# Three of the chunks' layer norms on ScalarE alone, and the first pair sums behind a product's outputs

## The chip, the cores and the metric

One core of one Trainium2 chip. The metric is the device time of one execution in microseconds (us); quoted times are medians of the runs of one kernel. The span of a profile, taken on one execution, is about 1.8 us shorter than that execution's time. Engines: PE is TensorE (PEld its weight loads), DVE is VectorE, ACT is ScalarE, POOL is GpSimd, SP is SyncE, which issues most of the DMAs here.

Some terms. A bank is one of the 8 PSUM buffers of the kernel's pool `psum`, which take PE's products; evacuating it means reading the product out, on ACT or DVE. `pg`, `pu`, `pv`, `ex` and `ey` are names of such products, `sg` is what ACT reads out of the q, k and v projection, and "a `pv` wait" is PE's wait before that product.

## The reference

A transformer block in bf16, 2048 rows of 1024, both layer norms before their part:

```python
h  = x + wo( local_attention( layernorm(x) @ wqkv ) )      # 32 heads, window 8, dilation 2
h2 = h + ( (layernorm(h) @ w_gate) * (layernorm(h) @ w_up) ) @ w_down     # w_gate, w_up: 1024 x 3584

def _layernorm(x, axis=-1, eps=1e-5):
    m = jnp.mean(x, axis=axis, keepdims=True)
    v = jnp.var(x, axis=axis, keepdims=True)
    return (x - m) / jnp.sqrt(v + eps)
```

## The kernel before: the parts that matter

The 2048 rows go through in four chunks of 512 (four tiles of 128 rows). Every engine's order is fixed by the program: `bg.step(us)` stands between PE's matmul groups and emits pieces of background work (attention and norms of other chunks), as far as a credit in microseconds allows. PE's order never changes. Chunks 2 and 3 are multiplied at the end with a scheme that needs sums and differences of weights and activations in fp16 (`weight_sums`, `activation_sums`).

A row tile's norm takes statistics on DVE, two small activations on ACT for the reciprocal deviation, a normalize on DVE and a DMA transpose that SP issues. In the output projection of a chunk that stands between the groups:

```python
lnp  = ctx.enter_context(tc.tile_pool(name="ln", bufs=4))
psum = ctx.enter_context(tc.tile_pool(name="psum", bufs=8, space=PSUM))
# ... cut ...
def stats(src, mv4, t):
    st = small.tile([128, 2, nc.vector.BN_STATS_DIM], F32, tag="st")
    for i in range(2):
        nc.vector.bn_stats(out=st[:, i, :], in_=src[:, bass.ts(i, 512)])
    nc.vector.bn_aggr(out=mv4[:, t, :], in_=st[:])

def rstd_of(mv4, rs4, lo, hi):
    nc.scalar.activation(rs4[:, lo:hi], mv4[:, lo:hi, 1], ACTF.Ln, bias=eps[:])
    nc.scalar.activation(rs4[:, lo:hi], rs4[:, lo:hi], ACTF.Exp, scale=-0.5)
# ... cut ...
def wo_ln2(c):
    lnT = lnTp.tile([128, KO, TC], BF, tag="lnT", name=f"lnT2_{c}")
    hs = hss[c]
    mv4, rs4 = ln_tiles(f"2_{c}")

    def norm(t):
        ln = normalize(hs[t], mv4, rs4, t)
        nc.sync.dma_start_transpose(lnT[:, :, bass.ts(t, 128)], ln[:])

    for t in range(4):
        for hf in range(2):
            ps = psum.tile([128, 512], F32, tag="mm", name=f"wo{c}_{hf}_{t}")
            # ... 8 matmuls into ps ...
            nc.vector.tensor_tensor(hs[t][:, bass.ts(hf, 512)], ps[:], hs[t][:, bass.ts(hf, 512)], ALU.add)
            if hf == 1:
                stats(hs[t], mv4, t)
                rstd_of(mv4, rs4, t, t + 1)
                bg.spend(1.5)
            elif t > 0:
                norm(t - 1)
                bg.spend(0.55)
            bg.spend(0.7)
            bg.step(GROUP_US)
    norm(3)
    retire(2)              # frees two weight buffers: SP issues the next two loads of 1 MB
    return lnT, hs
```

`ffn1(0, lnT2)` consumes `lnT`: its first group multiplies all 512 columns, so it waits for the last of the four transposes. The place of the pair sums, near the end of chunk 1's work:

```python
sub([dn["kx"], dn["vx"]], dn["21"], dn["11"])
weight_sums(0, nc.vector)
retire(2)
et = att.tile([128, TC], F32, tag="t3", name="et")
for q in range(2):
    dprod(ex[q], q, EF["21"], fcells(dn["12"]), False)
    nc.vector.tensor_tensor(et[:], p5t[:, q, :], hs1[2 + q][:, 512:1024], ALU.add)
    result(1, hs1[2 + q], 2 + q, 1, ex[q], dn["inv"], et)   # reads the bank ex[q] out, on DVE
retire(1)
activation_sums(l2, l3, dn["px"])
for q in range(2):
    dprod(ey[q], q, EF["12"], fcells(dn["22"]), False)
    nc.vector.tensor_tensor(p5t[:, q, :], p5t[:, q, :], hs1[q][:, 512:1024], ALU.add)
    result(1, hs1[q], q, 1, ey[q], dn["inv"], p5t[:, q, :])
for q in range(2):
    dprod(ex[q], q, EF["22"], fcells([dn["kx"], dn["vx"]]), False)
    # ... cut ...
```

Of the kernel before, what the change touches and what calls it, by code (L numbers as in the profile page):

```python
# [8 lines left out]
BF = mybir.dt.bfloat16  # L9
F32 = mybir.dt.float32  # L10
# [3 lines left out]
ACTF = mybir.ActivationFunctionType  # L14
# [4 lines left out]
D = 1024  # L19
# [6 lines left out]
TC = 512  # L26
NCH = S // TC
SUB = TC // 4
KO = D // 128
# [7 lines left out]
class Background:  # L37
# [3 lines left out]
    def __init__(self):  # L41
        self.items = []
        self.now = 0.0
        self.credit = 0.0
        self.rate = 1.0

    def add(self, gen, ready=0.0, first=False):
        self.items.insert(0 if first else len(self.items), [ready, gen])
# [3 lines left out]

    def step(self, us):
        self.now += us
        self.credit = min(self.credit + us * self.rate, 4.0)
        while self.credit > 0:
            item = next((i for i in self.items if i[0] <= self.now), None)
            if item is None:
                break
            try:  # L60
                got = next(item[1])
                if isinstance(got, tuple):
                    item[0] = self.now + got[1]
                else:
                    self.credit -= got
            except StopIteration:
                self.items.remove(item)

    def finish(self, gen):
        for item in self.items:  # L70
# [8 lines left out]
def kernel(  # L79
# [11 lines left out]
    nc = tc.nc  # L91
# [8 lines left out]
    lnTp = ctx.enter_context(tc.tile_pool(name="lnT", bufs=3))  # L100
# [21 lines left out]
    bg = Background()  # L122
# [35 lines left out]
    wts = {}  # L158
# [19 lines left out]
# [10 lines that stand above are left out]
    def normalize(src, mv4, rs4, t):  # L188
        ln = lnp.tile([128, D], BF, tag="ln")
        nc.vector.tensor_scalar(ln[:], src[:], mv4[:, t, 0:1], rs4[:, t:t + 1], ALU.subtract, ALU.mult)  # L190
        return ln

    def ln_tiles(name):
        mv4 = small.tile([128, 4, nc.vector.BN_AGGR_DIM], F32, tag="mv4", name="mv" + name)
        rs4 = small.tile([128, 4], F32, tag="rs4", name="rs" + name)
        return mv4, rs4
# [8 lines left out]

    lnTs = {}

    xtiles = {}

    class Norm1:  # L210
# [31 lines left out]
    def rows_gen(n, on_array):  # L242
        for t in range(6):
# [6 lines left out]
            if t > 1 and on_array:  # L250
                n.transpose_on_array(t - 2)
                yield 0.45

    def stats_gen(n):
        for t in range(4):
            n.stat(t)
            yield 1.5

    def norm_gen(n):
        for t in range(4):  # L260
            n.norm(t)
            n.transpose(t)
            yield 0.55


    x0 = [hp.tile([128, D], BF, tag="h", name=f"x0_{t}") for t in range(4)]
# [112 lines left out]
    xtiles[1] = load_x(1, "x", nc.sync)  # L379
    pump(4)  # L380
    xtiles[2] = load_x(2, "x", nc.sync)
    norm1 = {c: Norm1(c) for c in (1, 2, 3)}
    bg.add(rows_gen(norm1[1], True))
    rows2 = rows_gen(norm1[2], False)
    bg.add(rows2)
# [114 lines left out]
    def wo_ln2(c):  # L500
        lnT = lnTp.tile([128, KO, TC], BF, tag="lnT", name=f"lnT2_{c}")
        hs = hss[c]
        mv4, rs4 = ln_tiles(f"2_{c}")

        def norm(t):
            ln = normalize(hs[t], mv4, rs4, t)
            nc.sync.dma_start_transpose(lnT[:, :, bass.ts(t, 128)], ln[:])

        for t in range(4):
            for hf in range(2):  # L510
                ps = psum.tile([128, 512], F32, tag="mm", name=f"wo{c}_{hf}_{t}")
                for kk in range(KO):
                    nc.tensor.matmul(ps[:], lhsT=oTs[c][:, kk, t, :], rhs=wts["wo", c, hf][:, kk, :],  # L513
                                     start=(kk == 0), stop=(kk == KO - 1))
                nc.vector.tensor_tensor(hs[t][:, bass.ts(hf, 512)], ps[:], hs[t][:, bass.ts(hf, 512)], ALU.add)
                if hf == 1:
                    stats(hs[t], mv4, t)
                    rstd_of(mv4, rs4, t, t + 1)
                    bg.spend(1.5)
                elif t > 0:  # L520
                    norm(t - 1)
                    bg.spend(0.55)
                bg.spend(0.7)
                bg.step(GROUP_US)
        norm(3)
        retire(2)
        return lnT, hs

# [30 lines left out]
            nc.vector.tensor_scalar(ib[:], eb[:], float(12 << 23), None, ALU.subtract)  # L559
            self.s, self.inv = sb[:].bitcast(F32), ib[:].bitcast(F32)  # L560

    scale_gu, scale_d, scale_h = Scale("gu", 56), Scale("d", 56), Scale("h", 56)
    scale_h1 = Scale("h1", 28)

    def abs_sum(c, b, j):
# [2 lines left out]
        scale_gu.add(28 * c + 4 * b + j, wt[:, bass.ts(j, 2), :], junk[:])  # L568

    def abs_sum_down(hf, b, j):  # L570
        junk = lnp.tile([128, 512], BF, tag="ln", name=f"junkd{hf}_{b}_{j}")
        scale_d.add(28 * hf + 7 * b + j, wts["wd", 0, hf, b][:, j, :], junk[:])

    def abs_sum_h(n, k, ht):
        junk = lnp.tile([128, 512], BF, tag="ln", name=f"junkh{n}_{k}")
# [6 lines left out]
    def ffn1(c, lnT, at={}):  # L582
        hT = []
        for b in range(7):
            if b == 5 and c + 1 < NCH:
                hss[c + 1] = load_x(c + 1, "h", nc.sync)
            for j in range(4):
                pg = psum.tile([128, TC], F32, tag="mm", name=f"pg{c}_{b}_{j}")
                mm_group(pg, wts["wg", c, b], j, lnT)
                gs = t1k.tile([128, TC], BF, tag="t1k", name=f"gs{c}_{b}_{j}")  # L590
                nc.scalar.copy(gs[:], pg[:])  # L591
                bg.step(GROUP_US)
                pu = psum.tile([128, TC], F32, tag="mm", name=f"pu{c}_{b}_{j}")
                mm_group(pu, wts["wu", c, b], j, lnT)
                us = t1k.tile([128, TC], BF, tag="t1k", name=f"us{c}_{b}_{j}")
                nc.scalar.copy(us[:], pu[:])  # L596
                nc.vector.tensor_tensor(gs[:], gs[:], us[:], ALU.mult)
                abs_sum(c, b, j)
                bg.spend(0.45)
                bg.step(GROUP_US)  # L600
                hT.append(gs)
                if (b, j) in at:
                    at[b, j]()
                f = len(hT) - 3
                if c == 1 and f >= 0:
                    abs_sum_h1(f, hT[f])
            retire(2)
            if b in at:
                at[b]()
        if c == 1:  # L610
            for f in range(NF - 2, NF):
                abs_sum_h1(f, hT[f])
        return hT
# [6 lines left out]
    def ffn2(c, hf, hT, hs, between={}):  # L620
        acc = [psum.tile([128, 512], F32, tag="mm", name=f"acc{c}_{hf}_{t}") for t in range(4)]
        for b in range(4):
            for j in range(7):
                f = b * 7 + j
                for t in range(4):
                    nc.tensor.matmul(acc[t][:], lhsT=hT[f][:, bass.ts(t, 128)],  # L626
                                     rhs=wts["wd", c, hf, b][:, j, :],
                                     start=(f == 0), stop=(f == NF - 1))
                if c == 0:
                    abs_sum_down(hf, b, j)  # L630
                bg.step(0.86)
            retire()
            if b in between:
                between[b]()
        for t in range(4):
            ffn2_store(c, t, hf, acc[t], hs)
            bg.spend(0.7)
# [30 lines left out]
    def activation_sums(l2, l3, room):  # L668
        b11, b12, b21, b22 = l2[:, 0:4, :], l3[:, 0:4, :], l2[:, 4:8, :], l3[:, 4:8, :]

        t1, t2, t3, t4 = (room[:, bass.ts(i, 4), :].bitcast(F16) for i in range(4))
        nc.vector.tensor_tensor(t1, b12, b11, ALU.subtract)
        nc.vector.tensor_tensor(t2, b22, t1, ALU.subtract)
        nc.vector.tensor_tensor(t3, b22, b12, ALU.subtract)
        nc.vector.tensor_tensor(t4, b21, t2, ALU.subtract)
        pair["b"] = (b11, b21, t1, t2, t3, t4, b22)
# [56 lines left out]
        norm1[2].transpose(t)  # L733
    xtiles[3] = load_x(3, "x", nc.sync)
    pump(6)
    bg.add(stats_gen(norm1[3]), bg.now + 6.0)
    start_attention(0)
    qkv(1, range(4))
    qkv(0, range(4, 6))
    load_v(0)  # L740
    bg.add(norm_gen(norm1[3]), bg.now, first=True)
    qkv(1, range(4, 6))
    start_attention(1)
    pump(pair_at)
# [7 lines left out]
    qkv(3, range(4, 6), last=True)  # L752
    start_attention(3)
    lnT2, hs = nxt
    hT = ffn1(0, lnT2)
    bg.finish(atts[1])
    nxt = wo_ln2(1)
    for hf in range(2):
        ffn2(0, hf, hT, hs)
    lnT2, hs = nxt  # L760
    def f16(ap):
        return ap.bitcast(F16)

# [206 lines left out]
    for t in range(4):  # L970
        ln_rows(3, t, l3)
    sub([dn["kx"], dn["vx"]], dn["21"], dn["11"])
    weight_sums(0, nc.vector)
    retire(2)
    et = att.tile([128, TC], F32, tag="t3", name="et")
    for q in range(2):
# [2 lines left out]
        result(1, hs1[2 + q], 2 + q, 1, ex[q], dn["inv"], et)  # L979
    retire(1)  # L980
    activation_sums(l2, l3, dn["px"])
    for q in range(2):
        dprod(ey[q], q, EF["12"], fcells(dn["22"]), False)
        nc.vector.tensor_tensor(p5t[:, q, :], p5t[:, q, :], hs1[q][:, 512:1024], ALU.add)
        result(1, hs1[q], q, 1, ey[q], dn["inv"], p5t[:, q, :])
# [140 lines left out]
```

## Time and profile before

| | before |
|---|---|
| time, first three runs | 783.46 us median, 782.1 to 784.1 |
| profiled execution | span 779.9 us, mean granted clock 0.999 |
| PE, DVE, ACT busy | 98%, 79%, 61% of the span |
| longest wait of PE | 3.2 us, for DVE to read a bank out, at 511 |

PE is the bound. A busy share of 98% leaves 13 us of idle time in all, so this is read by place: where does PE stand still, and who ended it? An engine other than PE that stands still costs nothing by itself. The lines are in the prediction.

### The profile page before, as it was taken

How to read it: one execution, taken by the hardware profiler on the slowest of the kernel's cores; microseconds unless marked ns; L12 is line 12 of the kernel's file. 1: busy time of each engine (PE TensorE's matmuls, PEld its weight loads, DVE VectorE, ACT ScalarE, POOL GpSimd, SP SyncE). 2: the span in 40 equal slices, each digit the busy share in tenths (PEclk: the TensorE clock that was granted, in tenths of full speed). 3: DMA queues.
4: the chain of work that ended last, by engine and by line, in shares of the span. 5: the costliest groups of instructions: out<-in, count | busy, mean ns of one | idle time of the engine just before them, and what ended most of it. 6: DMA issues, size and time to landing. Idle time of an engine off the chain costs nothing.

```text
span 779.9 us, 10436 instructions
## 1 busy us (share of the span) xinstructions
PE 766.8 (98%) x3648; PEld 355.0 (46%) x3707; DVE 614.9 (79%) x805; ACT 473.5 (61%) x1028; POOL 142.4 (18%) x152
## 2 busy tenths in 40 slices
PE   8999999999999999999999999989999999999997
PEld 6544444444444444444444444434444444444444
DVE  6629999999899998999979989975553444579862
ACT  5627445313576652966769799836677677788240
POOL 0000000010000200002000001008778677600000
PEclk9999999999999999999999999999999999999999
DMA  8999693896955868858555492824332323730001
GB/s 272 260 236 209 169 274 90 262 274 173 341 174 186 297 215 234 270 189 270 195 163 195 133 313 75 183 74 110 106 99 64 108 67 97 255 123 28 1 27 55
DMA packets 181605, 133.86 MB, mean 172 GB/s; under 512 B 79024, under 2 KB 174384, under 8 KB 179504
## 3 DMA queue, kind: packets, MB, share of 16 engines
q1 hardware_dynamic: 177968, 111.17, 50.1%
q0 software_dynamic: 3584, 22.02, 8.1%
q8 instruction: 29, 0.48, 0.3%
q14 instruction: 24, 0.20, 0.1%
HBM read 104.86 MB, written 22.02 MB: 163 GB/s over the span
## 4 chain that ended last, share of the span: by engine, by line
PE 88%; DVE 9%; ACT 1%; issue 1%; DMA 1%; SPq 0%; DVEq 0%
PE ps L392 20%; PE pu L392 12%; PE pg L392 12%; PE dx L787 6%; PE pz L680 6%; PE acc L626 6%; PE py L680 6%; PE px L680 6%; PE wo L513 4%; PE pv L680 3%; PE dy L787 3%; DVE h L834 1%; PE ps L355 1%; PE ex L787 1%; DVE prodx L780 1%
## 5 line engine op out<-in xcount | busy, mean ns | idle before, releaser
L392 PE MATMUL ps<-lnT,w_qkv 128*128 128x512 bf16 x721 | 158.9, 379 | 0.8
L392 PEld LDWEIGHTS <-w_qkv 128*128 128x128 bf16 x736 | 71.9, 98 | 85.9
L392 PE MATMUL pu<-lnT,w_wu 128*128 128x512 bf16 x438 | 105.1, 379 | 0.6
L392 PE MATMUL pg<-lnT,w_wg 128*128 128x512 bf16 x440 | 105.1, 379 | 0.4
L306 ACT CAST sg<-ps 128x512 bf16<-128x512 f32 x96 | 54.8, 590 | 54.4 <-PE ps L392 51.1
L475 DVE TENSOR_TENSOR pv<-vD,at 128x4096 bf16<-128x4096 bf16 x32 | 72.5, 2287 | 0.3
L432 DVE TENSOR_TENSOR prod<-qD,kD 128x4096 bf16<-128x4096 bf16 x32 | 72.3, 2284 | 0.1
L680 PEld LDWEIGHTS <-sw 128*128 128x128 f16 x448 | 43.8, 98 | 53.2 <-issue 0.4
L392 PEld LDWEIGHTS <-w_wg 128*128 128x128 bf16 x448 | 43.8, 98 | 52.9
L392 PEld LDWEIGHTS <-w_wu 128*128 128x128 bf16 x448 | 43.8, 98 | 52.9
L596 ACT CAST us<-pu 128x512 bf16<-128x512 f32 x56 | 33.2, 593 | 41.1 <-PE pu L392 38.7
L680 PE MATMUL px<-lnT,ws 128*128 128x512 bf16 x212 | 53.1, 379 | 0.6
L680 PEld LDWEIGHTS <-ws 128*128 128x128 f16 x336 | 32.9, 98 | 39.6
L626 PE MATMUL acc<-w_wd,gs 128*128 128x512 bf16 x219 | 48.2, 379 | 0.3
L487 POOL DMA_DIRECT2D od<-oD x4 | 2.2, 544 | 252.3 <-DVE oD L485 162.5
L661 POOL TENSOR_TENSOR sw<-ws 128x512 f16<-128x512 f16 x26 | 30.0, 1154 | 87.6 <-PE py L680 80.4
L591 ACT CAST gs<-pg 128x512 bf16<-128x512 f32 x56 | 32.9, 587 | 11.4 <-PE pg L392 9.3
L185 ACT ACTIVATE rs<-mv,eps 128x1 f32<-128x1 f32 (+1 forms) x25 | 7.4, 297 | 50.3 <-DVE mv L182 47.1
L434 DVE TENSOR_TENSOR prod<-prod 128x4096 bf16<-128x4096 bf16 x16 | 36.6, 2288 | 0.3
L541 ACT ACTIVATE junkd<-w_wd 128x512 bf16<-128x512 bf16 x56 | 34.3, 613 | 0.0
L626 PEld LDWEIGHTS <-gs 128*128 128x128 bf16 x224 | 21.9, 98 | 26.4
L697 ACT COPY py<-px 128x512 f32<-128x512 f32 x28 | 16.0, 570 | 29.6 <-PE px L680 29.6
(304 smaller groups left out, 1398.0 us busy)
## 6 DMA issues: line engine op xcount, KB each, us to landing
w_wg<-in_B_w_gate_dram SPq DMA_DIRECT2D x14, 1024.0 KB, 6.6
w_wu<-in_B_w_up_dram SPq DMA_DIRECT2D x14, 1024.0 KB, 5.3
w_wd<-in_B_w_down_dram SPq DMA_DIRECT2D x8, 896.0 KB, 7.4
w_pair<-in_B_w_gate_dram SPq DMA_DIRECT2D x14, 512.0 KB, 4.0
w_pair<-in_B_w_up_dram SPq DMA_DIRECT2D x14, 512.0 KB, 5.2
w_wo<-in_A_wo_dram SPq DMA_DIRECT2D x6, 1024.0 KB, 8.4
w_qkv<-in_A_wqkv_dram SPq DMA_DIRECT2D x5, 1024.0 KB, 9.1
kd<-sg SPq DMA_DIRECT2D x32, 144.0 KB, 2.9
```

Source lines behind the costliest of these rows:

```text
L306: nc.scalar.copy(sg[:, HB:HB + TC], ps[:])
L392: nc.tensor.matmul(ps[:], lhsT=wt[:, ko, bass.ts(j, 128)], rhs=rhs[:, ko, :], start=(ko == 0), stop=(ko == KO - 1))
L432: nc.vector.tensor_tensor(prod[:, j], qD[:], kD[:, :, o:o + SUB], ALU.mult)
L434: nc.vector.tensor_tensor(prod[:, :, 0:16], prod[:, :, 0:16], prod[:, :, 16:32], ALU.add)
L475: nc.vector.tensor_tensor(pv[:, j], vD[:, :, o:o + SUB], at[:, w, None, :].to_broadcast((128, DH, SUB)), ALU.mult)
L513: nc.tensor.matmul(ps[:], lhsT=oTs[c][:, kk, t, :], rhs=wts["wo", c, hf][:, kk, :], start=(kk == 0), stop=(kk == KO - 1))
L541: nc.scalar.activation(junk, src, ACTF.Abs, accum_out=self.l1[:, k:k + 1])
L591: nc.scalar.copy(gs[:], pg[:])
L596: nc.scalar.copy(us[:], pu[:])
L626: nc.tensor.matmul(acc[t][:], lhsT=hT[f][:, bass.ts(t, 128)], rhs=wts["wd", c, hf, b][:, j, :], start=(f == 0), stop=(f == NF - 1))
L680: nc.tensor.matmul(ps[:], lhsT=lhs[:, ko, :], rhs=rhs[:, ko, :], start=(fresh and ko == 0), stop=(ko == 3), skip_group_check=not fresh)
L787: nc.tensor.matmul(ps[:, bass.ds(lo, n)], lhsT=lhs[k][:, bass.ts(q, 128)], rhs=rhs[k][:, bass.ds(lo, n)], start=(fresh and k == 0), stop=( ...
```

## The change

The intent, as the diff shows it: relieve DVE. The first norm of chunk 3 and the second norms of chunks 0 and 1 go to ACT, which sums, squares and normalizes with activations alone, in three pieces per row tile; one piece is emitted per step, in the output projection two per group. The sums over w_down's elements are taken in larger pieces. And the first pair sums on DVE move behind the outputs of a product.

```diff
+        self.rows = []
     def step(self, us):
         self.now += us
+        self.row_piece()
 ...
+    def row_piece(self):
+        while self.rows:
+            if next(self.rows[0], None) is not None:
+                return
+            self.rows.pop(0)
 ... (finish_rows: emits what is left)
+    def scalar_rows(src, lnT, t, name):
+        sm = small.tile([128, 5], F32, tag="am", name="am" + name)
+        total, nmean, squares, rstd, shift = (sm[:, i:i + 1] for i in range(5))
+        junk = lnp.tile([128, D], BF, tag="ln", name="jm" + name)
+        nc.scalar.activation(junk[:], src[:], ACTF.Copy, accum_out=total)
+        yield True
+        nc.scalar.activation(nmean, total, ACTF.Copy, scale=-1.0 / D)
+        junk = lnp.tile([128, D], BF, tag="ln", name="jv" + name)
+        nc.scalar.activation(junk[:], src[:], ACTF.Square, bias=nmean, accum_out=squares)
+        yield True
+        nc.scalar.activation(rstd, squares, ACTF.Ln, bias=eps[:], scale=1.0 / D)
+        nc.scalar.activation(rstd, rstd, ACTF.Exp, scale=-0.5)
+        nc.scalar.activation(shift, nmean, ACTF.Copy, scale=rstd)
+        ln = lnp.tile([128, D], BF, tag="ln", name="ln" + name)
+        nc.scalar.activation(ln[:], src[:], ACTF.Identity, bias=shift, scale=rstd)
+        nc.sync.dma_start_transpose(lnT[:, :, bass.ts(t, 128)], ln[:])
+        yield True
 ... (wo_ln2)
-                    stats(hs[t], mv4, t)
-                    rstd_of(mv4, rs4, t, t + 1)
-                    bg.spend(1.5)
-                elif t > 0:
-                    norm(t - 1)
-                    bg.spend(0.55)
+                    bg.rows.append(scalar_rows(hs[t], lnT, t, f"2_{c}_{t}"))
+                bg.row_piece()
                 bg.spend(0.7)
                 bg.step(GROUP_US)
-        norm(3)
         retire(2)
 ... (w_down's sums: 512 elements a piece -> 1024)
-                if c == 0:
+                if c == 0 and j % 2 == 0:
                     abs_sum_down(hf, b, j)
 ... (chunk 3's first norm)
-    bg.add(stats_gen(norm1[3]), bg.now + 6.0)
-    bg.add(norm_gen(norm1[3]), bg.now, first=True)
+    bg.rows += [scalar_rows(xtiles[3][t], lnTs[3], t, f"1_3_{t}") for t in range(4)]
 ... (both places that use a second norm: bg.finish_rows() before it)
-    weight_sums(0, nc.vector)
     retire(2)
     et = att.tile([128, TC], F32, tag="t3", name="et")
 ... (the loop over ex)
     activation_sums(l2, l3, dn["px"])
+    weight_sums(0, nc.vector)
```

A consequence that the diff does not say aloud: `retire(2)` still ends `wo_ln2`, but the last piece of row tile 3, with its transpose, is emitted later. So SP now issues two weight loads of 1 MB ahead of the fourth transpose.

More of the change, by code (lines that the diff above doesn't have):

```diff
@@ L67, in step, with finish_rows @@
                 self.items.remove(item)
+    def row_piece(self):
[3 more added lines that the diff above has]
+            self.rows.pop(0)
+    def finish_rows(self):
+        for gen in self.rows:
+            for _ in gen:
+                pass
+        self.rows = []
     def finish(self, gen):
@@ L252, in rows_gen @@
                 yield 0.45
-    def stats_gen(n):
-        for t in range(4):
-            n.stat(t)
-            yield 1.5
-    def norm_gen(n):
-        for t in range(4):
-            n.norm(t)
-            n.transpose(t)
-            yield 0.55
     x0 = [hp.tile([128, D], BF, tag="h", name=f"x0_{t}") for t in range(4)]
@@ L381 @@
     xtiles[2] = load_x(2, "x", nc.sync)
-    norm1 = {c: Norm1(c) for c in (1, 2, 3)}
+    norm1 = {c: Norm1(c) for c in (1, 2)}
     bg.add(rows_gen(norm1[1], True))
@@ L502, in wo_ln2 @@
         hs = hss[c]
-        mv4, rs4 = ln_tiles(f"2_{c}")
-        def norm(t):
-            ln = normalize(hs[t], mv4, rs4, t)
-            nc.sync.dma_start_transpose(lnT[:, :, bass.ts(t, 128)], ln[:])
         for t in range(4):
@@ L560, in total @@
             self.s, self.inv = sb[:].bitcast(F32), ib[:].bitcast(F32)
-    scale_gu, scale_d, scale_h = Scale("gu", 56), Scale("d", 56), Scale("h", 56)
+    scale_gu, scale_d, scale_h = Scale("gu", 56), Scale("d", 32), Scale("h", 56)
     scale_h1 = Scale("h1", 28)
@@ L570, in abs_sum_down @@
     def abs_sum_down(hf, b, j):
-        junk = lnp.tile([128, 512], BF, tag="ln", name=f"junkd{hf}_{b}_{j}")
-        scale_d.add(28 * hf + 7 * b + j, wts["wd", 0, hf, b][:, j, :], junk[:])
+        n = min(2, 7 - j)
+        junk = lnp.tile([128, n, 512], BF, tag="ln", name=f"junkd{hf}_{b}_{j}")
+        scale_d.add(16 * hf + 4 * b + j // 2, wts["wd", 0, hf, b][:, j:j + n, :], junk[:])
     def abs_sum_h(n, k, ht):
@@ L740 @@
     load_v(0)
-    bg.add(norm_gen(norm1[3]), bg.now, first=True)
+    lnTs[3] = lnTp.tile([128, KO, TC], BF, tag="lnT", name="lnT1_3")
+    bg.rows += [scalar_rows(xtiles[3][t], lnTs[3], t, f"1_3_{t}") for t in range(4)]
     qkv(1, range(4, 6))
@@ L754 @@
     lnT2, hs = nxt
+    bg.finish_rows()
     hT = ffn1(0, lnT2)
@@ L760 @@
     lnT2, hs = nxt
+    bg.finish_rows()
     def f16(ap):
```

## The prediction

> **What bounds the kernel now.** First the busy times of the page.
>
> ```profile
> PE 766.8 (98%) x3648; PEld 355.0 (46%) x3707; DVE 614.9 (79%) x805; ACT 473.5 (61%) x1028; POOL 142.4 (18%) x152
> ```
>
> TensorE (PE) is busy for 766.8 of 779.9 us, at a granted clock of 0.999. A change that leaves the matmuls alone can win at most the other 13.1 us. The table of busy time by stretch (PE is the second number) says where these lie.
>
> ```profile
> 0.00:25.00 25.00, 22.57 (x217) 14.71 (x219) 14.96 (x36) 13.23 (x32) 1.62 (x16) 1.00 0.87 292
> 25.00:160.00 135.00, 134.32 (x632) 61.90 (x643) 113.74 (x102) 63.36 (x200) 7.47 (x11) 1.00 0.82 211
> 160.00:192.00 32.00, 31.84 (x147) 14.50 (x149) 30.87 (x38) 8.96 (x30) 0.00 (x0) 1.00 0.75 202
> ...
> 500.00:533.00 33.00, 29.56 (x135) 13.30 (x136) 23.46 (x36) 15.98 (x18) 6.45 (x6) 1.00 0.53 120
> ...
> 690.00:780.00 90.00, 85.63 (x409) 39.73 (x407) 63.34 (x132) 39.85 (x53) 0.00 (x0) 0.99 0.14 45
> ```
>
> PE is idle for 2.4 us at the start, 3.4 in 500 to 533, 4.4 in the last stretch, 2.9 in all the rest. The change touches neither start nor end. So the most that it can give is about 3.4 us, 0.4%. The waits of PE name them as one wait, the longest of all:
>
> ```profile
> PE ex L787 <- DVE h L792: 3.2, 1, 3.2
> ```
>
> The timelines of PE and of VectorE (DVE) there:
>
> ```profile
> 509.70 1.67 PE L787 MATMUL ey<-lx,gs 128*128 128x512 f16 x7
> 514.56 1.67 PE L787 MATMUL ex<-kx,gs 128*128 128x512 f16 x7 [3.18 <-DVE h L792]
> ```
>
> ```profile
> 510.42 0.69 DVE L661 TENSOR_TENSOR sw<-ws 128x1024 f16<-128x1024 f16 x1 [4.44 <-ACT ws L654]
> 512.96 0.68 DVE L978 TENSOR_TENSOR et<-ep,h 128x512 f32<-128x512 f32 x1
> 513.75 0.75 DVE L792 SCALAR_TENSOR_TENSOR h<-ex,inv_h1d,et 128x512 bf16<-128x512 f32 x1
> ```
>
> PE had both ex products by 505.2 and wants to accumulate new ones in these banks from 511.4. But DVE, in order, sits at the first pair sums (L661 to L664): idle 4.4 us until ScalarE (ACT) has scaled their weights, then 2.5 us of sums, before it reads ex out.
>
> **The second place** is quiet before, and the change works there: the first output projection (PE 163.5 to 177.3), whose layer norm feeds ffn1 at 191.1. In it ACT waits for DVE's statistics; the last row is normalized at 186.4 and its DMA transpose issued by 187.8 (SP's timeline), so the norm is ready some 1.5 us early.
>
> ```profile
> 175.74 0.30 ACT L185 ACTIVATE rs<-mv,eps 128x1 f32<-128x1 f32 x1 [11.35 <-DVE mv L182]
> ...
> 185.72 0.57 ACT L306 CAST sg<-ps 128x512 bf16<-128x512 f32 x1
> ```
>
> ```profile
> 176.88 10.91 SPq L507 DMA_TRANSPOSE lnT<-ln  x4
> ```
>
> ```profile
> 191.13 1.89 PE L392 MATMUL pg<-lnT,w_wg 128*128 128x512 bf16 x8
> ```
>
> ACT stood still 11.4 us there and 9.2 us at 106 (an exp waiting for DVE), and PE lost nothing: such pauses fit in the PSUM banks.
>
> ```profile
> 106.14 1.06 ACT L452 ACTIVATE lg<-lg 128x1024 f32<-128x1024 f32 x1 [9.19 <-DVE lg L451]
> 107.10 3.98 ACT L306 CAST sg<-ps 128x512 bf16<-128x512 f32 x8
> ```
>
> **What the Trainium skill says.** "ScalarE: Activation LUTs", section "What ACT_TABLE_LOAD costs": an activation with immediates takes 186 ns + 0.833 ns per element, each pointer operand adds about 93 ns, neighbours overlap by 93. For 1024 elements: 1.04, 1.13, 1.22 us. The trace agrees (copy, square with a bias, identity with bias and scale):
>
> ```profile
> 482.23 1.06 ACT L850 ACTIVATE lnjunk<-h 128x1024 bf16<-128x1024 bf16 x1
> ...
> 488.02 1.15 ACT L857 ACTIVATE lnjunk<-h,lnroom 128x1024 bf16<-128x1024 bf16 x1
> ...
> 493.87 1.24 ACT L869 ACTIVATE lnr<-h,lnroom,rs 128x1024 bf16<-128x1024 bf16 x1 [1.50 <-DVE lnroom L864]
> ```
>
> The same page, "Table sets": Ln and Exp share the set that the kernel preloads, and cheap functions are in every set; so no table loads are added. "PSUM — Partial Sum Buffer", section "PSUM: the matmul accumulator": 8 banks; a projection group takes PE 1.73 us here, so evacuation may stand still for roughly 12 us (estimate, 7 x 1.73), which fits the two pauses. "DMA: Bandwidth & Descriptors", section "Queues, rings and completion order": the transfers of SP share one row of rings, consumed in ring order; a transpose behind weight loads therefore lands late. In the trace transposes land in 3.2 us (median), and in 8.8 at worst.
>
> **The change part by part.** PE's instructions are the same 7416 in the same order.
>
> *Removed from DVE*: for 12 row tiles two statistics (1.28 us together), one aggregate (0.21), one normalize (0.5): 12 x 2.0 = 24 us busy. DVE 615 to about 591. No PE wait hung on these: 0 us.
>
> *Added to ACT*: per row copy 1.06, square 1.15, identity 1.24, two accumulator reads 0.19, Ln 0.30, Exp 0.20, two tiny copies 0.20 and 0.28 = 4.8 us; 12 rows 58 us, less the 12 old Ln/Exp pairs (6 us). The sums of w_down go in pieces of 1024: 56 x 0.613 = 34.3 becomes 24 x 1.06 + 8 x 0.61 = 30.3. ACT 473.5 to about 521. All of it lies beside PE, if the banks and the norms come in time.
>
> *Chunk 3's norm*: ACT does 12 pieces in 12 steps from 83 us. Three steps take it 3 x 0.80 of evacuation + 4.4 of pieces = 6.8 against PE's 5.2, so by 104 it is some 8 us behind, at most 6 banks full: no wait. DVE starts the first attention when kD has landed (issued 42.5, 8.8 to 9.6 us to land: about 51.7) instead of 59.5, and skips 1.8 us of normalizing; but its exp now stands in ACT's queue behind eight pieces, until 100.2 + 1.1. DVE is then 5.9 us earlier than before, not 9.6.
>
> *Chunk 0's second norm*: 5.9 us earlier DVE has h of row 0 at 170.9 (before: 174.2). ACT then runs four rows with nothing between: start to start a row is 1.18 + 0.24 + 1.27 + 0.33 + 0.24 + 0.24 + 1.14 = 4.64. Three rows: 184.9; row 3's copy and square: 187.4; one evacuation that stands between (0.58): 188.0; its last piece: 190.0. Before: 186.4. The transpose lands 3.2 later, 193.2, and PE wants it at 191.1: a new wait of 2 us. SP's order makes it worse: two loads of 1 MB now stand before the fourth transpose, not behind it (issued from 186; 2 MB at about 300 GB/s, the best slice of the page, is 7 us). If the transpose queues fully behind them it lands near 196. If my ACT times are 2 us too long there is no wait. I take 2 us, between 0 and 5.
>
> *Chunk 1's second norm* runs from about 292 to 312, needed at 350: free. The weight sums behind it end at about 342 (before 343.4).
>
> *The pair sums moved*: after the subtraction at 506.0 DVE runs straight on to et and ex: ex is free at about 509, before 511.4. The 3.18 us go. Then the activation sums, when the last transposed rows have landed (about 510): 4 x 1.17 to 515; pair sums 2.55 to 517.4. PE, now 3.2 earlier, wants them for pv at 519.1. The second pv needs the bank that the next result frees, at about 520.9, and wants it at 520.9: hardly a wait. Gain 3.0, between 2 and 3.3.
>
> Sum: 783.5 - 3.0 + 2.0 = 782.5. Since the two pieces per group look like a remedy against just that late norm, I lean a little to the side where it comes in time: 782.0.
>
> **Rivals.** (1) The norm is in time and only the gain stays: 780.3. For it: DVE gets earlier, and before there was 1.5 us of slack. Against: ACT needs 18.6 us for four rows in a row, DVE needed 12. (2) The late norm costs more than the sums give: 4 to 6 us of new wait, 784.5 to 786.5. For it: the two loads ahead of the transpose. Against: with fewer waits on DVE, the rows may start sooner than 170.9. (3) ACT becomes the bound and the banks fill in steps 41 to 57. For it: 8 us behind. Against: 10 us of pause were taken before without loss. It would add 1 to 3 us. (4) DVE's relief speeds up the whole: against it, PE has no other wait on DVE worth 1 us. Not above 0.5 us.
>
> **Range and chances.** The gain is capped at 3.4, so 779.5 is a floor but for noise (runs of before spread from 782.1 to 784.1); rival 2 sets the top. 8 in 10: 779.3 to 785.8. A 2% change is 15.7 us: nothing found comes near it. Faster 0.01, same 0.97, slower 0.02.
>
> **What would show it.** The 3.2 us wait of PE on L792 gone, pair sums after the activation sums; ACT near 521 and DVE near 591 us busy; ACT's first big idle (9.2 before the exp) gone, DVE waiting for that exp instead; the last row of the first second norm ending near 190, with a PE wait of 0 to 5 us on the transpose at 191. Wrong: a PE wait on evacuations (L306) near 105 or 185, or more than 5 us lost at 191, or a new wait at the first pair block.

## More of the kernel before

The granted clock is the share of its full clock that TensorE was given, as the profile records it; "half clock" is a record of 0.50.

The flight of a DMA is the time from its issue to its landing.

## The result, and the profile after

| | before | after |
|---|---|---|
| time, median | 783.59 us (782.1 to 784.1, 4 runs) | 789.49 us (788.5 to 790.05, 4 runs) |
| span of the profiled run | 779.9 us | 787.5 us |
| mean granted clock of it | 0.999 | 0.993 |

The ratio is 1.0077, with a 95% interval from 1.006 to 1.0095: slower by 0.8%. A ratio here is the mean time of one kernel's fast runs over the mean of the other's of the same rounds, so it is not quite the ratio of the medians.

The page of the kernel after, engine, busy us, share, instructions:

```profile
PE 773.3 (98%) x3707; PEld 356.0 (45%) x3707; DVE 593.4 (75%) x757; ACT 516.8 (66%) x1064; POOL 142.1 (18%) x152
```

DVE was relieved as intended, 21 us, and ACT loaded with 43. Busy shares tell nothing of what follows. PE's waits, of the same kernel (total us, times, longest):

```profile
PE pg L414 <- DMA lnT<-ln: 7.4, 1, 7.4
...
PE pv L692 <- DVE h L807: 0.9, 2, 0.6
```

The wait for `ex` is gone; in its place stands one of 7.4 us for a transpose. PE's timeline where ffn1 starts (start us, duration, then the idle time before it and what ended it):

```profile
198.56 3.57 PE L414 MATMUL pg<-lnT,w_wg 128*128 128x512 bf16 x8 [7.41 <-DMA lnT<-ln]
201.93 2.91 PE L414 MATMUL pu<-lnT,w_wu 128*128 128x512 bf16 x8
204.68 1.89 PE L414 MATMUL pg<-lnT,w_wg 128*128 128x512 bf16 x8
```

From start to start the first product takes 3.37 us, the second 2.75, a usual one 1.73 (before's products follow at that pace). Of 2.66 us more the clock is the cause, as a stretch of one microsecond in the table of busy times shows (PE is full, the granted clock, third number from the right, is 0.50):

```profile
199.00:200.00 1.00, 1.00 (x4) 0.40 (x3) 1.00 (x1) 0.00 (x0) 0.00 (x0) 0.50 1.28 199
```

PE's busy time of 773.3 instead of 766.8 is therefore no extra work. The trace of before lacks some records (3648 matmuls shown there, 3707 here); pair_fill below, whose trace has all 3707 of the same matmuls, shows 770.3, and the slow products (2.7) make up most of the difference of 3.0.

Why the transpose was late is read from SP's timeline, then from the chain of waits that ends in that product:

```profile
176.03 12.00 SPq L238 DMA_TRANSPOSE lnT<-ln  x3
188.12 0.53 SPq L181 DMA_DIRECT2D w_wu<-in_B_w_up_dram  x1
188.75 0.53 SPq L181 DMA_DIRECT2D w_wg<-in_B_w_gate_dram  x1
189.37 1.46 SPq L341 DMA_DIRECT2D vd<-sg  x1
190.93 4.73 SPq L238 DMA_TRANSPOSE lnT<-ln  x1
```

```profile
180.75 8.62 DMA lnT<-ln
...
190.93 7.50 DMA lnT<-ln
198.43 0.14 issue
198.56 3.57 PE pg L414 x8
```

The last row's normalize ended at 190.7 on ACT, the transpose was issued at 190.93 and landed 7.5 us later. Two megabytes of weights stood in the same queue from 188.1 on; the second of these loads (issued at 188.75, flight 8.2) landed at 197.0, the transpose 1.5 us after it. The second transpose, too, took 8.6 us (it stands in this chain because ACT's last normalize began right after it landed, but ACT was idle for only 0.15 us there): then the queries and keys of chunk 2 were being loaded, which POOL had asked for when DVE became free for the next attention. On POOL's timeline that is at 178.7, where the kernel before, in the second line here, had it at 194.67:

```profile
178.70 0.55 POOL L434 DMA_DIRECT2D qD<-qd  x1 [27.76 <-DVE prod L454]
194.67 0.55 POOL L412 DMA_DIRECT2D qD<-qd  x1 [35.95 <-DVE prod L432]
```

**The account between the two profiled runs.** New wait +7.4; products at half clock +2.7; wait for `ex` −3.2; waits for `pv` +0.7 (0.85 instead of 0.16). Sum +7.6, as the spans say (787.5 − 779.9).

### The profile page after: what moved, and what is told of

The parts are those of the page before. It is cut to its first block, busy times and chain, and to the rows that moved or that the text cites. A ratio compares the mean times of both kernels' runs of the same rounds, so it can differ in the third digit from the quotient of the medians.

```text
span 787.5 us, 10469 instructions
## 1 busy us (share of the span) xinstructions
PE 773.3 (98%) x3707; PEld 356.0 (45%) x3707; DVE 593.4 (75%) x757; ACT 516.8 (66%) x1064; POOL 142.1 (18%) x152
## 4 chain that ended last, share of the span: by engine, by line
PE 84%; DVE 10%; DMA 3%; ACT 1%; issue 1%; SPq 0%; DVEq 0%; ACTq 0%
PE ps L414 18%; PE pg L414 13%; PE pu L414 12%; PE dx L802 6%; PE pz L692 6%; PE acc L638 6%; PE py L692 6%; PE px L692 6%; PE pv L692 3%; PE dy L802 3%; PE wo L529 2%; DMA lnT<-ln 2%; DMA prodx<-in_B_w_down_dram 1%; DVE h L849 1%; PE ps L377 1%
## 5 line engine op out<-in xcount | busy, mean ns | idle before, releaser
L414 PE MATMUL pg<-lnT,w_wg 128*128 128x512 bf16 x448 | 107.5, 383 | 7.4 <-DMA lnT<-ln 7.4
L414 PE MATMUL pu<-lnT,w_wu 128*128 128x512 bf16 x448 | 106.9, 382 | 0.0
L692 PE MATMUL px<-lnT,ws 128*128 128x512 bf16 x224 | 55.2, 379 | 0.0
L609 DVE TENSOR_TENSOR gs<-gs,us 128x512 bf16<-128x512 bf16 x56 | 23.5, 419 | 33.2 <-ACT us L608 33.2
L674 POOL TENSOR_TENSOR sw<-sw,ws 128x512 f16<-128x512 f16 x26 | 30.0, 1152 | 2.0
```

What stands on the lines that cost most here:

```text
L414: nc.tensor.matmul(ps[:], lhsT=wt[:, ko, bass.ts(j, 128)], rhs=rhs[:, ko, :], start=(ko == 0), stop=(ko == KO - 1))
L674: eng.tensor_tensor(sw[:, i, 1], sw[:, i, 0], a11, ALU.subtract)
L692: nc.tensor.matmul(ps[:], lhsT=lhs[:, ko, :], rhs=rhs[:, ko, :], start=(fresh and ko == 0), stop=(ko == 3), skip_group_check=not fresh)
```

## The experiments

The theory: PE's loss at 191 comes from the second norm of chunk 0 alone. ACT ends its four rows late, and then the fourth transpose lands late because it stands behind two loads. Rivals: the earlier loads of q and k hold the transposes; ACT's held-up evacuations of banks would make PE wait anyway; the other two norms on ACT cost something. All runs gave correct results.

### pair_only: only the pair sums moved

```diff
  sub([dn["kx"], dn["vx"]], dn["21"], dn["11"])      # kernel before
- weight_sums(0, nc.vector)
  retire(2)
  ...
  activation_sums(l2, l3, dn["px"])
+ weight_sums(0, nc.vector)
```

> Kernel before with only the first pair sums moved behind the activation sums. Theory (the move is worth the 3.18 us wait, less what comes back at the first pair block, where the changed kernel shows waits of 0.63 and 0.22): 2.3 to 3.2 us faster than before, the wait of PE on the results of ex gone. Rival (the gain of the move exists only together with the earlier VectorE of the rest of the change): within 1 us of before.

Measured: 779.79 us against 783.58, ratio 0.9954 [0.994, 0.9967]. The 3.2 us wait is gone; a small one took its place:

```profile
PE pv L680 <- DVE h L792: 0.8, 2, 0.6
```

This half of the change wins 3.6 us by the ratio (0.0046 x 783), more than the net wait of 2.5 (3.18 less 0.63 more for `pv`). The rest is put down to the clock. The runs of the kernel before fall into two groups: 10 runs at a mean granted clock of 0.999 or 1.0 took 782.2 us on average, 19 at 0.998 or less took 784.1. Every run of the versions without a long wait (this one, first_norm_dve, pair_fill, mixed_fill: 21 runs) had 0.999 or 1.0. So the 3.2 us pause of the kernel before seems to bring the half clock in some two thirds of its runs, at 1.9 us each, 1.2 on average. The profile that was shown is one of the fortunate third. That the slow clock falls just there is inferred from the averages; no trace of such a run was taken.

### first_norm_dve: the changed kernel with chunk 0's second norm on DVE again

```diff
+ on_dve = c == 0                     # in wo_ln2
+ if on_dve: (stats, rstd_of, norm as before)
- if hf == 1:
+ elif hf == 1:
      bg.rows.append(scalar_rows(hs[t], lnT, t, f"2_{c}_{t}"))
```

> The changed kernel with chunk 0's second layer norm back on VectorE, all else of the change kept. Theory (all of the loss, 7.4 us of wait and some 2.7 us at half clock after it, comes from that one norm on ScalarE): no PE wait at the start of ffn1, no half clock, 2.3 to 3.2 us faster than before, about 10 us faster than the changed kernel. Rival (the other two norms on ScalarE, or their traffic, cost as well): slower than before less 2 us.

Measured: 780.8 us, ratio 0.9964 [0.9951, 0.9978]. No wait at 191; the clock 1.0 throughout. So of the change's ratio of 1.0077, the one norm makes 0.0113, some 8.9 us. The theory holds in the main; the norms of chunks 1 and 3 and w_down's pieces cost some 0.8 us (the ratio less that of pair_only), which mixed_fill below takes up. What was not expected: a `pv` wait of 1.5 us, since the last transposed rows landed later and DVE's activation sums with them.

### loads_after: the two loads issued behind the fourth transpose

```diff
      nc.sync.dma_start_transpose(lnT[:, :, bass.ts(t, 128)], ln[:])     # in scalar_rows
+     if name == "2_0_3":
+         retire(2)
  ...
- retire(2)                                                              # end of wo_ln2
+ if c > 0:
+     retire(2)
```

> The changed kernel with the two 1 MB weight loads of SP issued behind the fourth transpose instead of before it. Theory A (the transpose is late because it stands behind these loads in the rings): it lands some 3.2 us after issue, the PE wait falls from 7.4 to about 3, the half clock shrinks or goes, 4 to 7 us faster than the changed kernel. Rival B (it is late because of the q and k loads of the next chunk, which a freer VectorE now lets start at 178.7 instead of 194.7): within 1 us of the changed kernel.

Measured: 784.54 us, ratio 1.0007 [0.999, 1.0025], about 5 us better than after. SP's and PE's timelines:

```profile
191.65 1.24 SPq L238 DMA_TRANSPOSE lnT<-ln  x1
192.98 0.53 SPq L181 DMA_DIRECT2D w_wu<-in_B_w_up_dram  x1
```

```profile
194.89 3.41 PE L416 MATMUL pg<-lnT,w_wg 128*128 128x512 bf16 x8 [2.73 <-ACT sg L330]
```

The fourth transpose alone, asked by its tile (window 191 to 194):

```profile
L238 SPq DMA_TRANSPOSE lnT<-ln x1: 1238/1238/1238, 191.6 to 191.6; - x1
DMA to landing us min/median/max: 3.1/3.1/3.1
```

Issued 0.7 us later than in after, the transpose landed 3.7 us earlier: its flight was 3.1 us instead of 7.5. The order in SP's queue is the main cause, worth some 5 us of the 8.9; the other 3.4 (ratio less that of first_norm_dve, times 783) stay with ACT's late rows and what follows from them.

The wait of 2.7 us that is left is still one for this transpose, although the timeline names ACT's `sg`, an evacuation of a bank. The landing (191.65 + 3.1; 194.76 in the trace's record of the semaphore) comes 0.13 us before PE's product, just as in after (198.43 and 198.56), where ACT had no evacuation under way. PE's product also waits on a counter of ACT's progress, which was updated in between, at 194.82, and the profile names the update that came last. PE had ended its projections at 192.16, and the transpose was issued only at 191.65, since ACT ends its four rows late. So the rival of held-up evacuations is not shown by this run.

### qk_held: chunk 2's q and k loaded only after the fourth transpose

```diff
  # in load_qk; lnT2s[0] is chunk 0's transposed norm
+ if c == 2:
+     nc.gpsimd.tensor_copy(qD[:, 0, 0:1], lnT2s[0][:, 0, TC - 1:TC])
  nc.gpsimd.dma_start(qD[:], qd[c].rearrange("c g d s -> (c g) d s"))
```

> The changed kernel with the q and k loads of chunk 2 held until the fourth transpose has landed (GpSimd first copies one column of the transposed tile). Theory A (the weight loads make the transpose late): within 1 us of the changed kernel. Rival B (these loads make it late): second transpose lands in 3 to 4 us instead of 8.6, the fourth in about 3.2, PE wait about 3, 4 to 7 us faster than the changed kernel. If both share the rings' bandwidth, something between: 1 to 4 us faster.

Measured: 787.85 us, ratio 1.0053 [1.0033, 1.0072]. The chain and PE:

```profile
191.30 6.48 DMA lnT<-ln
```

```profile
197.91 3.30 PE L414 MATMUL pg<-lnT,w_wg 128*128 128x512 bf16 x8 [5.44 <-DMA lnT<-ln]
```

The q and k loads are worth about 1 us of the fourth transpose's flight (6.5 instead of 7.5) and 1.6 us of time by the medians; the greater part of the delay stays. (PE's wait is 2.0 us shorter, since the issue also came earlier: 1.2 us before PE's wait began, in after 0.2.) The second transpose, which in after flew beside these loads, takes 3.1 us here instead of 8.6, so to it they were worth 5.5 us; but PE waits for the last of the four. The Trainium skill, "DMA: Bandwidth & Descriptors", section "Issuing engines are not separate DMA queues", says that transfers from any engine run on the same 16 DMA engines and interleave; the run agrees, with that 1 us and those 5.5 us as its sizes here.

### both: loads_after and qk_held together

> Loads of weights behind the fourth transpose and the q and k loads held until it has landed, both. Theory (without either, the transpose lands in 3.2 us, and what is left is ScalarE's lateness: with the weight loads moved alone PE waited 2.7 us for ScalarE's evacuations of PSUM, not for the transpose): PE still waits 2 to 3 us at the start of ffn1, within 1 us of the run with the weight loads alone moved. Rival (the q and k loads held back the evacuations too): the wait falls under 1 us, 2 us or more faster than that run.

Measured: 783.97 us, ratio 1.001 [0.9991, 1.0028], the same as loads_after within the noise: once the transpose is out from behind the loads, no further cost of q and k is seen in the time. The expectation took the wait of loads_after for one on evacuations, as the timeline has it. It is the late transpose here, too, as SP's timeline and the answer for its tile (window 191.5 to 194) show:

```profile
191.84 1.24 SPq L238 DMA_TRANSPOSE lnT<-ln  x1
DMA to landing us min/median/max: 3.1/3.1/3.1
```

```profile
195.09 3.47 PE L416 MATMUL pg<-lnT,w_wg 128*128 128x512 bf16 x8 [2.23 <-ACT sg L333]
```

The landing (194.96 in the semaphore's record) again comes 0.13 us before PE's product; the ACT instruction that the timeline names is another one than in loads_after.

### chunk3_dve: the changed kernel with chunk 3's first norm on DVE again

```diff
- bg.rows += [scalar_rows(xtiles[3][t], lnTs[3], t, f"1_3_{t}") for t in range(4)]
+ bg.add(stats_gen(norm1[3]), bg.now + 6.0)
+ bg.add(norm_gen(norm1[3]), bg.now, first=True)       # at their places of before
```

> The changed kernel with chunk 3's first layer norm back on VectorE, the other two on ScalarE. Theory (the start of ScalarE's four rows is set by when VectorE has the sums h, and the rows run in series from there): h of row 0 ready some 3 us later (174 instead of 171), the fourth transpose and so the PE wait 2 to 4 us longer, 2 to 4 us slower than the changed kernel. Rival (chunk 3's norm on ScalarE is itself part of the loss, through the exp that it holds up or the earlier q and k loads): faster than the changed kernel by 1 us or more.

Measured: 794.87 us, ratio 1.0153 [1.0136, 1.0169]. Expected was 2 to 4 us of loss, it was 5.4. SP's timeline and the chain:

```profile
196.40 4.88 SPq L238 DMA_TRANSPOSE lnT<-ln  x1
```

```profile
196.40 7.66 DMA lnT<-ln
```

With chunk 3's norm on DVE, DVE delivers the first row of h later, so that ACT starts it at 175.56 instead of 171.19; SP comes to its fourth transpose 5.5 us later (one load's issue took 3.5 us on SP, where it usually takes 0.5; why was not looked into), and PE's wait grows to 12.3 us. So the norm of chunk 3 on ACT does help: it makes the late norm of chunk 0 less late. By itself it gives nothing, as mixed_fill below shows.

### gap_filled: dummy matmuls in the wait

```diff
  # in ffn1, before the group of pg
+ if c == 0 and b == 0 and j == 0:
+     for i in range(33):
+         nc.tensor.matmul(pg[:], lhsT=ident[:], rhs=wts["wg", 0, 0][:, i % KO, :], start=True, stop=True)
  mm_group(pg, wts["wg", c, b], j, lnT)
```

> The changed kernel with 33 matmuls (33 x 0.216 = 7.1 us) that compute nothing of use put into TensorE's wait at the start of ffn1, in the bank that the first product overwrites. Theory (the wait also costs some 2.7 us because TensorE runs at half the granted clock for 5 us after it): the granted clock stays at 1.00 there, the first two products take 1.73 us each instead of 3.4 and 2.7, and the kernel is 1.5 to 3 us faster than the changed kernel although it does more work. Rival (the first products are slow for another reason, such as contention of their operands with the loads): the products stay slow, within 1 us of the changed kernel.

Measured: 788.52 us, ratio 1.0072 [1.0052, 1.0091]. In the profile the first products took 1.73 us each, so the half clock is indeed the answer to PE's pause. The dummies themselves delayed nothing: the transpose, issued at 191.56, took 7.5 us, and the real work began at 199.26. But the time hardly fell: this profile had 1.8 us of `pv` waits (after: 0.9) and 1.5 us of waits for the first weights at its start, which after's had not. Inconclusive as to the time, so it was repeated below on a base without the `pv` waits.

### pair_fill: pair_only with two sums pulled ahead

```diff
  retire(1)                            # on pair_only
+ for q in range(2):
+     nc.vector.tensor_tensor(p5t[:, q, :], p5t[:, q, :], hs1[q][:, 512:1024], ALU.add)
  activation_sums(l2, l3, dn["px"])
  weight_sums(0, nc.vector)
  for q in range(2):
      dprod(ey[q], q, EF["12"], fcells(dn["22"]), False)
-     nc.vector.tensor_tensor(p5t[:, q, :], p5t[:, q, :], hs1[q][:, 512:1024], ALU.add)
```

> The kernel before with the pair sums moved (which alone gave 0.9954 of before) and the two sums of p5 with the residual (0.68 us each) pulled ahead of the activation sums, into the 1.95 us in which VectorE waits there for the last transposed rows. Theory (the 0.63 and 0.22 us that PE lost at the first pair block hung on the results behind these sums): those waits gone, 0.5 to 0.9 us faster than the pair sums moved alone. Rival (the two sums push the activation sums back by as much): no faster, waits as before.

Measured: 778.88 us against 783.42, ratio 0.9946 [0.9931, 0.996]: the fastest version here, ahead of both kernels. DVE does the two sums while it would wait for the last transposed rows, and the `pv` waits are gone.

### after_fill and gap_fill: the dummies once more

Both are the changed kernel with the two sums pulled ahead as in pair_fill; gap_fill has the 33 dummy matmuls too.

> The changed kernel with the two sums of the output tile pulled ahead of the activation sums, as in pair_fill. Only a base for gap_fill: the waits for pv (0.9 us in the profile of after) should go, so about 0.7 us under after: 788.8, ratio 1.007 to before; the wait of 7 us on the fourth transpose and the half clock behind it stay.

> after_fill with 33 dummy matmuls in the wait for the fourth transpose, as in gap_filled, now without the waits for pv that hid its effect. Theory (half clock costs 2.7 us by itself): the first products take 1.73 us each; the dummies end up to 0.9 us after the landing, so the net is 1.6 to 2.7 us faster than after_fill, ratio 1.0035 to 1.005 to before. Rival (the slow products are absorbed by some later slack, or cost nothing on the path): within 0.7 us of after_fill.

Measured: after_fill 787.73 us, ratio 1.006 [1.0044, 1.0076]; gap_fill 786.78, ratio 1.0046 [1.0033, 1.0059]. PE's timeline of after_fill, then of gap_fill:

```profile
197.91 3.50 PE L414 MATMUL pg<-lnT,w_wg 128*128 128x512 bf16 x8 [6.44 <-DMA lnT<-ln]
201.24 1.89 PE L414 MATMUL pu<-lnT,w_wu 128*128 128x512 bf16 x8
```

```profile
191.31 7.29 PE L603 MATMUL pg<-w_wg,ident 128*128 128x512 bf16 x33
198.44 1.89 PE L414 MATMUL pg<-lnT,w_wg 128*128 128x512 bf16 x8
200.17 1.89 PE L414 MATMUL pu<-lnT,w_wu 128*128 128x512 bf16 x8
```

after_fill came out 1.1 us under what was expected: it had 1 us less of wait than after, and only one slow product: 3.33 us from start to start, 1.6 too many. With dummies the real work began 0.53 us later, because in that profile the transpose was issued 0.24 us later and flew 7.8 us instead of 7.5; its second product began 1.07 us earlier all the same (200.17 against 201.24). The measured gain is 1.1 us by the ratios (0.0014 x 783), 0.95 by the medians, between what the theory (1.6 at least) and the rival (0.7 at most) expected, and the two intervals overlap. The two profiles show no gain in their spans (784.7 and 785.0), because gap_fill's has a `pv` wait of 1.3 us that after_fill's has not. So at this place the half clock costs time of its own, 1.6 us after this pause and 2.7 in the profile of after; that a part of it reaches the total is what the 1.1 us say, and how much of it does stays open.

### mixed_fill: chunk 0's norm on DVE, the other two on ACT, the sums pulled ahead

> The changed kernel with chunk 0's second norm back on VectorE and the two sums pulled ahead: keeps ScalarE's norms of chunks 1 and 3, the w_down pieces of 1024, the moved pair sums. Theory (the first norm is the only part of ScalarE's norms that acts, the other two are free and give nothing): the time of pair_fill, 778.9, ratio 0.994 to 0.9955. Rival (the relief of VectorE is worth something once the late norm is gone): under 777.9, ratio below 0.993. Rival (ScalarE's norms of chunks 1 and 3 cost something): over 780, ratio over 0.996.

Measured: 779.68 us, ratio 0.9957 [0.9943, 0.9972]. That is pair_fill within 0.0011, just past the edge of what the theory expected and inside neither rival. The norms of chunks 1 and 3 on ACT and the larger w_down pieces win nothing; if anything they lose some 0.8 us (one `pv` wait of 0.9 us stands in this profile), which these intervals do not settle.

## Why the prediction was wrong

Predicted were 782.0 us, between 779.3 and 785.8, a gain of 1.5; the kernel took 789.49, a loss of 5.9. Within 2%, as held nearly certain, it stayed. The steps, in the order of the prediction:

- **PE bounds the kernel, the gain is capped at 3.4 us.** Right as far as the profile went. Part of the idle time that was summed is missing records (in 25 to 160 before shows 134.32 us busy with 632 matmuls, after 135.00 with 645). The cap was taken from one profiled run at a clock of 0.999; the usual run of before loses some more to the clock, so pair_fill's ratio gives 4.2 us (0.0054 x 783).
- **The pair sums give 3.0, "hardly a wait" at the second pv.** pair_only: 3.6, with 0.6 us more of `pv` waits and about 1.2 of clock that no line of the one profile showed.
- **Chunk 3's norm: no wait of PE.** Right. The exp stood at 100.64 (predicted 100.2), DVE waited 4.8 us for it, PE was busy for all of 25 to 160, and h of row 0 came at about 171.2 (170.9). No table load was added: ACT's one load stands at 0.75 us in both traces.
- **Chunk 1's norm is free.** No PE wait behind it in the profile; mixed_fill, which has it, is within 0.9 us of pair_fill by the ratios.
- **ACT near 521, DVE near 591.** 516.8 and 593.4.
- **Chunk 0's norm: row 3's last piece ends at 190.0.** 190.7, right within a microsecond.
- **"The transpose lands 3.2 later, 193.2 ... a new wait of 2 us."** This step failed, in the flight of the transpose. The 3.2 was the median of before's transposes; before's fourth, which took 3.2 too, went out ahead of the two loads. The prediction named the two loads now ahead of the fourth, worked out 196, and still took 2 us, "between 0 and 5", in its sum. The flight was 7.5 us: the transpose landed at 198.4 and PE waited 7.4. loads_after shows what the order in the queue costs: with it undone the flight is 3.1. qk_held shows about 1 us of it for q and k. Even the 196 was too early, because it let the loads start at 186; they were issued at 188.1, and from there the prediction's own sum gives 188.1 + 7 + 3.2 = 198.3 (an estimate, checked by this one case). The other part of the term, ACT's lateness, was about right: with the loads behind the transpose PE waited 2.7 us (loads_after) and 2.2 (both), where the prediction had 2. The wait on evacuations that it listed as a sign of being wrong is not shown by any run.
- **No term for the clock.** The prediction priced a wait at its length. This wait brought the half clock for one to two products, 1.6 to 2.7 us more.
- **Slips in its sums that decided nothing.** 783.5 less 3.4 is 780.1, not the floor of 779.5. 5.9 us before 174.2 is 168.3; the 170.9 is given without working, though it came true. The traces show 2 x 3707 = 7414 instructions of PE, not 7416. And rival 2 reached 786.5, beyond the range that it was said to set.

By ratios the change divides into −3.6 (pair sums), +0.8 (the norms of chunks 1 and 3 with w_down's pieces, first_norm_dve less pair_only) and +8.9 (chunk 0's norm): +6.1, as measured (0.0077 x 783 = 6.0). The parts hold in this order only: with chunk 3's norm back on DVE, chunk 0's costs more (chunk3_dve). Rival 2, the late norm, was the right mechanism, put at 4 to 6 us and in truth 8.9. The lean to the side where the norm comes in time, because "two pieces per group look like a remedy", was a guess about intent, and against the trace: the pieces fix the order in which ACT works, while ACT's own 4.6 us a row and SP's queue set when the last row lands.

## What to carry to other kernels

When work moves to an engine that finishes it later, follow the data to the last DMA and look at what that DMA now stands behind in its queue: here the same transpose took 3.1 or 7.5 us by its place in the queue. A wait that the profile puts down to one engine may belong to another that ended just before: compare both with the time at which work resumes. If a program emits pieces later than the code around them, the issue of loads in that code moves ahead of them; issue what is waited for first, what is prefetched after. And price a pause of TensorE at more than its length, and take the clock of several runs, not of one, before calling a bound a bound.

## What the Trainium skill lacked or had wrong

- "TensorE: Matmul & The Clock Gate", section "HAM oscillation — how this bites in real kernels", gives the rule "no PE-idle gaps >~3.4µs", and the part that it belongs to has a free-running window. Here pauses of 2.2 and 2.7 us (both, loads_after) were followed by a half clock, at 3.3 and 3.2 us from start to start for a product of 1.73, while one of 3.18 us (the profile of before) was not. That the outcome varies from run to run fits a free-running window (loads_after had one run of four at 1.0 and 782.76 us, three at 0.997 or 0.998 and 784.4 to 784.9); the length in the rule does not fit.
- "DMA: Bandwidth & Descriptors", section "Queues, rings and completion order", has the order within a row of rings, but no figure for what a transpose loses behind loads: 7.5 us from issue to landing behind two loads of 1 MB, 3.1 ahead of them, 6.5 behind them with q and k held back.
- The same page, section "Issuing engines are not separate DMA queues", says that the transfers interleave, but gives no size. POOL's loads of q and k cost a transpose on SP's queue about 1 us here of 7.5 for the fourth, and 5.5 of 8.6 for the second, which flew beside them (after against qk_held).
